# Bulk transfers held until the planner's account of the queue is short: order on SP, and what follows from it

## The chip, the cores and the metric

The kernel runs on one core of a Trainium2 chip. Its engines are TensorE (PE; PEld is its weight load), VectorE (DVE), ScalarE (ACT), GpSimd (POOL) and SyncE (SP), which here issues nearly all transfers. The metric is the device time of one execution in microseconds, the median of several runs; lower is better.

## The reference

Attention whose scores are mixed over the heads before and after the softmax, then one expert layer:

```
scores = q @ k^T / 8                  # batch 4, 12 heads, 448 positions, head size 64
scores = mix over heads (w_pre)
attn   = softmax(scores)
attn   = mix over heads (w_post)
x      = attn @ v                     # 1792 tokens x 768
h      = x @ w_in                     # 768 x 2048
g      = h * clip(h + 3, 0, 6) / 6
out    = g @ w_out                    # 2048 x 768
```

All inputs are float32. w_in and w_out come as 64-bit words and are decoded on the chip.

## The kernel before

**Attention.** The query rows of a batch are cut into 8 tiles m of 60 rows (32 tiles in all). For a tile, three *score products* (line 448, p = 0 to 2) write a pair of PSUM banks, of which there is one; ACT empties it into a tile s (line 473), and SP copies s in four transfers (line 480) into T, where the heads lie side by side. Even m go to T_two, odd m to T_one. Then steps of ten rows follow, numbered s = 0 to 179 (45 a batch) and mostly taken two at a time under the first one's number. Such a step has a *pre mix* of T on PE (line 533), the negative maximum nb on DVE (line 541), the exponential e with its sum on ACT (line 542), the scaling by the sum on POOL, a split of e into two float16 parts eh and el (ACT, POOL), the *post mix* on PE (line 570, 48 matmuls), and the writing of its result into AR by ACT and DVE. After every twelve of them or so comes the *product with v* (line 607), which gives x for the next tokens. PE has six single banks for everything else than the score products.

**The expert layer.** The tokens make eight groups G of 240 or 208. For a group, 16 products of x with w_in (line 828, 18 matmuls each, in the program mostly chained to blocks of 72) give g: ACT (line 841) and DVE (line 843) evacuate, and SP stores two of them at a time from a ring of three tiles to a buffer in DRAM (line 846, gd). These *MoE blocks* are put between the steps of attention.

**w_out.** From step 72 on, every four steps one of 24 pieces of w_out (512 KB) is loaded into a ring of two (`bulk`), decoded by ACT and DVE in a ring WF of four places, and combined with others into seven sums P1 to P7, each stored to DRAM (`w_store`, lines 778 and 781). The last stage (line 1109) loads these sums and g again and makes seven products in place of eight.

**What sets the order.** The program first collects all operations with an engine, a duration, the tiles they read and write, and a priority (smaller goes first). `Plan.schedule` then plays them through: an engine that is free takes, of the operations whose inputs are ready at that time, the one of lowest priority. For a transfer it keeps an account of the queue: `bw["SP"]` is the time at which all that is queued will have moved, at 302 GB/s, and the landing is that time plus a latency. The resulting order is what the program issues. On the chip each engine runs its instructions in this order and waits for the semaphores of their inputs only; no times of the planner exist there.

Priorities that matter: a score copy has about the first step of the tile before its own, less 6; a load of w_out has its step plus 8, keys, queries and v of a batch lie between 30 steps before its first and one behind it; a g store has 20 for the first seven groups and a store of a w_out sum its step plus 10 or 11. So a g store stood ahead of every score copy of a later step.

Of the kernel before, what the change touches and what calls it, by code (L numbers as in the profile page):

```python
# [63 lines left out]
Z_AT = 30  # L64
LAT_0, ACT_T = 1.0, 1
S_BUFS, LAT_T, LAT_B = 3, 2.0, 3.0


class Op:
    __slots__ = ("eng", "dur", "fn", "prio", "n", "succ", "order", "ready", "end", "bytes", "no", "mode", "takes", "then", "share", "lat", "st")  # L70


class Buf:
# [46 lines left out]
class Plan:  # L120
# [11 lines left out]
    def __init__(self):  # L132
        self.ops, self.bufs, self.filler = [], {}, None

    def op(self, eng, dur, fn, r=(), w=(), prio=0.0, after=(), nbytes=0, mode=0, share=False, lat=1.0, st=None):
        o = Op()
        o.lat, o.st = lat, dur if st is None else st
        o.share = share or eng == "POOL"
        o.eng, o.dur, o.fn, o.prio, o.bytes, o.mode = eng, dur, fn, prio, nbytes, mode
        o.succ, o.order, o.n, o.ready, o.no, o.end, o.takes, o.then = [], [], 0, 0.0, len(self.ops), None, [], None  # L140
        deps = {}

        def need(d):
            deps[d.no] = d

        for x in r:
            b, key = x if isinstance(x, tuple) else (x, None)
            for k, u, wr in b.uses:
                if wr and (k is None or key is None or k == key):
                    need(u)  # L150
        for x in w:
            b, key = x if isinstance(x, tuple) else (x, None)
            if b.pool and not b.uses and b not in o.takes:
                o.takes.append(b)
            if b not in self.bufs:
                self.bufs[b] = []
            self.bufs[b].append(o)
            for k, u, wr in b.uses:
                if k is None or key is None or k == key:
                    need(u)  # L160
        for u in after:
            need(u)
        for x, wr in [(x, False) for x in r] + [(x, True) for x in w]:
            b, key = x if isinstance(x, tuple) else (x, None)
            b.uses.append((key, o, wr))
        for d in deps.values():
            d.succ.append(o)
            o.n += 1
        self.ops.append(o)
        return o  # L170
# [14 lines left out]
    def schedule(self, prio, stay):  # L185

        free, wait, ready, out = {}, {}, {}, []
        bw, mode, then = {"SP": 0.0, "ACT": 0.0}, None, None
        recent = collections.deque([(0.0, 0.5, 0.5)], 60)
        for o, n in zip(self.ops, self.counts):  # L190
            o.n, o.ready, o.end = n, 0.0, None
        for p in self.places:
            p.held = [None] * len(p.makes)
        port = {"DVE": 0.0, "POOL": 0.0}

        def push(o):
            if o.eng == "PE":
                ready["PE"].append((prio[o.no], o.no, o))
            else:
                heapq.heappush(wait[o.eng], (o.ready, o.no, o))  # L200

        for o in self.ops:
            if o.eng not in free:
                free[o.eng], wait[o.eng], ready[o.eng] = 0.0, [], []
            if o.n == 0:
                push(o)

        def release(s, t):
            s.ready = max(s.ready, t)
            s.n -= 1  # L210
            if s.n == 0:
                push(s)

        def avail(o):
            t = o.ready
            for p in {b.pool for b in o.takes}:
                x = p.ready(sum(b.pool is p for b in o.takes), self.HOP)
                if x is None:
                    return None
                t = max(t, x)  # L220
            return t

        while True:
            best = None
            for e in free:
                if e == "PE":
                    at = [(avail(x[2]), x) for x in ready[e]]
                    at = [(x, z) for x, z in at if x is not None]
                    if not at:
                        continue  # L230
                    t = max(free[e], min(at)[0])
                elif ready[e]:
                    t = free[e]
                elif wait[e]:
                    t = max(free[e], wait[e][0][0])
                else:
                    continue
                if best is None or t < best[0]:
                    best = (t, e)
            if best is None:  # L240
                break
            t, e = best
            if e == "PE":
                at = [(avail(x[2]), x) for x in ready[e]]
                at = [x for z, x in at if z is not None and z <= t + 1e-9]
                x = min(at)
                x = min([z for z in at if z[2] is then] or [z for z in at if z[2].mode == mode and z[0] < x[0] + stay] or [x])
                then = x[2].then
                ready[e].remove(x)
                o = x[2]  # L250
                fill = self.filler(free[e], t, recent, o) if self.filler else (0, None, 0.0)
                for b in o.takes:
                    b.pool.take(b, self.HOP)
            else:
                while wait[e] and wait[e][0][0] <= t + 1e-9:
                    o = heapq.heappop(wait[e])[2]
                    heapq.heappush(ready[e], (prio[o.no], o.no, o))
                o = heapq.heappop(ready[e])[2]
            o.end = t + o.dur
            if o.share:  # L260
                other = port["POOL" if e == "DVE" else "DVE"]
                o.end += self.SHARE[e] * max(0.0, min(o.dur, other - t))
                port[e] = o.end
            if e == "PE":
                n, fn, z = fill
                if fn is not None:
                    out.append((free[e], fn))
                o.end += z
                recent.append((free[e], t + z, self.FILL * n))
                recent.append((t + z, o.end, o.st))  # L270
            if e == "PE":
                o.end += self.SWITCH * (mode not in (None, o.mode))
                mode = o.mode
            free[e] = o.end
            if o.bytes:
                x, d, other = max(bw[e], t + 1.1), o.bytes / self.DMA_RATE, "ACT" if e == "SP" else "SP"
                both = min(d, max(0.0, bw[other] - x))
                bw[e], bw[other] = x + d + both, bw[other] + both
                o.end = bw[e] + o.lat
            out.append((t, o))  # L280
            for s in o.order:
                release(s, t)
            for s in o.succ:
                release(s, o.end + (0.0 if s.eng == o.eng == "PE" else self.PE_HOP if o.eng == "PE" else self.HOP))
        if sum(isinstance(o, Op) for _, o in out) < len(self.ops):
            return None, out
        return max(o.end for o in self.ops), out
# [17 lines left out]
def body(ctx: ExitStack, tc: tile.TileContext, q4, kT, vj, wpre0, wpost0, ident0, w_in, w_out, outT):  # L305
    nc = tc.nc
    PE, ACT, DVE, POOL, SP = nc.tensor, nc.scalar, nc.vector, nc.gpsimd, nc.sync
# [14 lines left out]
    plan = Plan()  # L322
# [20 lines left out]
    def pe(dur, fn, r, w, prio, after=(), mode=0, st=None):  # L343
        return plan.op("PE", dur, fn, r, w, prio, after, 0, mode, st=st)

    def dma(nbytes, fn, r, w, prio, after=()):
        return plan.op("SP", 0.5, fn, r, w, prio, after, nbytes)

    def dmas(nbytes, out, src, w, prio, after=()):
        return plan.op("SP", 0.5, lambda: SP.dma_start(out(), src), [], w, prio, after, nbytes)  # L350

    def bulk(nbytes, out, src, w, prio, after=()):
        q = BULK
        return plan.op(q, 0.5 if q == "SP" else 0.4, lambda: (SP if q == "SP" else ACT).dma_start(out(), src), [], w, prio, after, nbytes, lat=LAT_B)

    def amax(dst, src):
        DVE.tensor_reduce(dst, src, axis=AX.X, op=ALU.max, apply_absolute_value=True)
# [417 lines left out]

    def w_store(name, i, t, at):
        d = ws_dram[name, i] = Buf(lambda: dram.tile([P, 4 * P], F32, name=f"wsd_{name}_{i}"))
        dma(262144, lambda: SP.dma_start(d(), t()), [t], [d], at)

    def w_sum(out, x, y, op, at):  # L780
        dve(0.69, lambda: DVE.tensor_tensor(out(), x(), y(), op=op), [x, y], [out], at, True)
# [28 lines left out]
    g_dram = [Buf(lambda b=b: dram.tile([P, NFC, S], F32, name=f"gd_{b}")) for b in range(B)]  # L810

    def moe1(G, fcs):
        b, gi = divmod(G, 2)
        n, t0 = GTOK[gi], 240 * gi
        x = x_sb[G]
        at = 5000 + 100 * G
# [3 lines left out]
        for fc in fcs:  # L820
# [12 lines left out]
            r = lambda gt=gt, fc=fc: gt()[:, fc % 2, :n]  # L833
# [10 lines left out]
                                                                                op0=ALU.min, op1=ALU.mult), [ps, (six, fc)], [(gt, fc % 2)], -80)  # L844
            if fc % 2:
                dma(P * 8 * n, lambda fc=fc, gt=gt: SP.dma_start(g_dram[b]()[:, fc - 1:fc + 1, t0:t0 + n], gt()[:, :, :n]), [gt],
                    [(g_dram[b], (fc // 2, gi))], 20 if G < 7 else -500)

# [264 lines left out]
    def out(b, m, half, o):  # L1115
        e = m
        dma(P * 4 * NH, lambda: SP.dma_start(outT[e * P:(e + 1) * P, b * S + half * NH:b * S + half * NH + NH], o()), [o], [], 20)
# [111 lines left out]
```

## Time and profile before

| | |
|---|---|
| median of 3 runs | 797.99 us (795.62 to 799.82) |
| profiled execution, its own time | 803.97 us |
| its span | 802.2 us |
| mean granted TensorE clock | 0.991 |
| PE busy | 779.3 us (97%) |
| PEld busy | 631.3 us (79%) |
| DVE / ACT / POOL busy | 580.3 / 528.1 / 367.7 us |
| moved | 147.75 MB, mean 184 GB/s |
| score copies, issued by SP | 186 to T_two, 240 to T_one |

PE is busy when any matmul is in flight; matmuls overlap, and their ends are modelled. Each engine works in its program order, so an instruction that waits holds all behind it on its engine. Attention with the MoE blocks in it runs until about 580 us, the last stage from there to the end; the stretches of the next-to-last section are chosen along this line. The granted clock is TensorE's, as a share of its full speed.

### The profile page before, as it was taken

To read this page: it belongs to the slowest core of one execution; us is meant where nothing else is said; L and a number is where in the kernel's file an instruction comes from. 1 tells how busy PE (TensorE), PEld (TensorE's weight loads), DVE (VectorE), ACT (ScalarE), POOL (GpSimd) and SP (SyncE) were. 2 spreads that over 40 slices of the span, in tenths; PEclk is the share of its full clock that TensorE was granted. 3 is DMA by queue.
4 is the path that set the end of the run, shared out by engine and by line. 5 is a ranking of instruction groups with operands and counts; after the bars stand their busy time and mean duration, and the time that the engine had idled before them with its cause. 6 is when DMAs were issued, how large, how long until landed. Compare 5 with 4: busy or idle time off the path is not lost.

```text
span 802.2 us, 28025 instructions
## 1 busy us (share of the span) xinstructions
PE 779.3 (97%) x11616; PEld 631.3 (79%) x11616; DVE 580.3 (72%) x1152; ACT 528.1 (66%) x1044; POOL 367.7 (46%) x535
## 2 busy tenths in 40 slices
PE   6999999999999999999999989999999999999998
PEld 2566576577677768777788758768999999999998
DVE  2798886688969357778856776785678688989622
ACT  2487888698998647988775785886577465324200
POOL 2357789579988316777552665766200000000000
PEclk9999999999999999999999998999999999999999
DMA  7866653676364577665657666643699855654101
GB/s 231 228 185 188 200 173 107 217 235 206 96 188 152 160 226 250 221 187 171 206 164 255 202 199 208 188 126 119 180 287 364 292 170 175 187 170 146 41 14 52
DMA packets 100815, 147.75 MB, mean 184 GB/s; under 512 B 9840, under 2 KB 79824, under 8 KB 100688
## 3 DMA queue, kind: packets, MB, share of 16 engines
q1 hardware_dynamic: 100268, 145.31, 58.5%
q8 instruction: 91, 1.49, 0.8%
q10 hardware_dynamic: 420, 0.65, 0.3%
q14 instruction: 36, 0.29, 0.1%
HBM read 76.02 MB, written 31.20 MB: 134 GB/s over the span
## 4 chain that ended last, share of the span: by engine, by line
PE 77%; DVE 7%; DMA 5%; ACT 5%; POOL 2%; issue 2%; SPq 2%; ACTq 0%; POOLq 0%; DVEq 0%
PE single L1109 24%; PE single L828 21%; PE single L570 9%; PE single L607 8%; PE pair L448 7%; PE single L533 6%; PE single L873 3%; DVE nb L541 2%; DMA T_two<-s 2%; ACT e L542 1%; DMA wo<-in_w_out 1%; POOL e L551 1%; DMA T_one<-s 1%; ACT s L473 1%; SPq L480 1%
## 5 line engine op out<-in xcount | busy, mean ns | idle before, releaser
L828 PEld LDWEIGHTS <-wi 128*128 128x128 f16 x2304 | 213.0, 98 | 24.0 <-issue 18.3
L828 PE MATMUL single<-x,wi 128*128 128x208 f16 (+1 forms) x2304 | 228.6, 259 | 1.0 <-DVE AR L579 0.6
L554 POOL TENSOR_TENSOR el<-e,eh 128x448 f16<-128x448 f32 x156 | 166.9, 1089 | 41.5 <-ACT eh L553 39.7
L551 POOL TENSOR_SCALAR e<-e,r 128x448 f32<-128x448 f32 x180 | 129.4, 729 | 38.7 <-DVE r L545 29.4
L1109 PEld LDWEIGHTS <-ws_P 128*128 128x128 f16 x1440 | 138.0, 98 | 0.0
L542 ACT ACTIVATE e<-single,nb 128x448 f32<-128x448 f32 x180 | 113.7, 640 | 26.3 <-DVE nb L541 25.6
L541 DVE TENSOR_REDUCE nb<-single 128x1 f32<-128x448 f32 x180 | 103.5, 615 | 19.1 <-PE single L533 13.5
L841 ACT ACTIVATE g<-single,three,uh 128x240 f32<-128x240 f32 (+1 forms) x128 | 69.3, 542 | 50.9 <-PE single L828 50.3
L553 ACT ACTIVATE eh<-e 128x448 f16<-128x448 f32 x156 | 87.5, 583 | 14.3 <-POOL e L551 13.7
L448 PE MATMUL pair<-ks,qx 64*64 64x448 f32 x728 | 88.8, 552 | 4.5 <-ACT s L473 4.5
L473 ACT ACTIVATE s<-pair 128x896 f32<-128x896 f32 x90 | 82.7, 918 | 14.6 <-PE pair L448 7.8
L843 DVE SCALAR_TENSOR_TENSOR g<-g,six,single 128x240 f32<-128x240 f32 (+1 forms) x128 | 56.3, 442 | 39.9 <-ACT g L841 39.0
L570 PEld LDWEIGHTS <-eh 60*128 60x128 f16 x2496 | 66.2, 100 | 22.2 <-issue 21.0
L607 PEld LDWEIGHTS single<-AR,v 128*64 128x64 f32 (+1 forms) x1536 | 70.4, 140 | 14.2 <-issue 6.3
L607 PE MATMUL single<-AR,v 128*64 128x120 f32 (+3 forms) x1536 | 76.0, 270 | 0.7 <-ACT e L542 0.5
L570 PE MATMUL single<-wpost_h,eh 60*128 60x60 f16 x1248 | 72.2, 202 | 0.2 <-DVE x L633 0.2
L570 PE MATMUL single<-wpost_h,el 60*128 60x60 f16 x1248 | 72.2, 202 | 0.0
L570 PE MATMUL single<-wpost_l,eh 60*128 60x60 f16 x1248 | 71.9, 202 | 0.0
L1109 PE MATMUL single<-gx_P,ws_P 128*128 128x224 f16 x720 | 69.3, 259 | 0.0
L579 DVE TENSOR_SCALAR AR<-single 128x480 f32<-128x480 f32 (+1 forms) x92 | 58.2, 640 | 14.8 <-PE single L570 14.5
L581 ACT ACTIVATE AR<-single 128x480 f32<-128x480 f32 (+1 forms) x92 | 53.6, 585 | 22.5 <-PE single L570 22.0
L544 POOL TENSOR_SCALAR sm<-sm 128x2 f32<-128x2 f32 (+1 forms) x92 | 26.1, 284 | 84.3 <-ACT e L542 79.0
(240 smaller groups left out, 1161.4 us busy)
## 6 DMA issues: line engine op xcount, KB each, us to landing
T_two<-s SPq DMA_DIRECT2D x186, 105.0 KB
T_one<-s SPq DMA_DIRECT2D x144, 105.0 KB
wi<-in_w_in SPq DMA_DIRECT2D x16, 768.0 KB
wo<-in_w_out SPq DMA_DIRECT2D x24, 512.0 KB
wsd_P<-WF SPq DMA_DIRECT2D x42, 256.0 KB
wP<-wsd_P SPq DMA_DIRECT2D x36, 256.0 KB
gd<-g SPq DMA_DIRECT2D x32, 240.0 KB
gd<-g SPq DMA_DIRECT2D x32, 208.0 KB
```

What stands on the lines that cost most here:

```text
L448: PE.matmul(at[u]()[cc * D:cc * D + D], q()[r, o:o + D], ks_[cc]()[r, pr % 3, :], start=True, stop=True)
L473: act(0.9, lambda: ACT.activation(st(), two()[:, :, :S], AF.Copy), ps, [(st, 0), (st, 1)], at + 0.5)
L541: dve(0.53, lambda r=r: DVE.tensor_reduce(nb()[:, r:r + 1], ps[r]()[:, :S], axis=AX.X, op=ALU.max, negate=True), [ps[r]], [(nb, r)], s + 0 ...
L542: act(0.62, lambda r=r: ACT.activation(e()[:, r], ps[r]()[:, :S], AF.Exp, bias=nb()[:, r:r + 1], accum_out=sm()[:, r:r + 1]), [ps[r], (nb, ...
L551: pool(0.63, lambda r=r: POOL.tensor_scalar(e()[:, r], e()[:, r], rr()[:, r:r + 1], 1.0, op0=ALU.mult, op1=ALU.mult), [rr], [(e, r)], s + ...
L553: act(0.47, lambda r=r: ACT.activation(eh()[:, r], e()[:, r], AF.Copy), [(e, r)], [(eh, r)], s + 0.65 + 0.3 * r)
L554: pool(1.02, lambda r=r: POOL.tensor_tensor(el()[:, r], e()[:, r], eh()[:, r], op=ALU.subtract), [(e, r), (eh, r)], [(el, r)], s + 0.7 + 0 ...
L570: PE.matmul(out, x()[rows, r, js], z()[rows], start=(i == 0), stop=(i == len(mix) - 1))
L607: PE.matmul(pss[run]()[u * D:(u + 1) * D, k:k + N], v()[rows, jc, g * D:(g + 1) * D], cols(jc * H + g, rows), start=start, stop=stop)
L828: PE.matmul(pv(), wi_g[g]()[:, w, f0, cc, :], x()[:, z, cc, :n], start=(cc == 0 and i == 0), stop=(cc == 5 and i == 2))
L841: act(0.44, lambda fc=fc, pv=pv, r=r: ACT.activation(r(), pv(), AF.Relu, bias=three()[:, fc:fc + 1], scale=uh()[:, fc:fc + 1]), [ps, (thre ...
L1109: PE.matmul(ps()[:, :NH], w_view(w, y, 2 * m + i)[:, f], g(x)[:, f, :], start=(i == 0 and f == 0 and (y, x) == (0, 0)), stop=(i == 1 and f ...
```

## The change

An operation may carry a `hold` in microseconds. When the planner is about to take it, and the account says that the queue will still be at work for more than `hold` beyond the usual start of a transfer (1.1 us), it is put back to the time at which only `hold` is left; others that are ready go in the meantime. Both holds are 2.0 us. HOLD_IN goes to loads by `bulk` of priority over 100: keys, queries and v of later batches and the later pieces of w_out. HOLD_OUT goes to all stores of w_out's sums and to the g stores of the first seven groups. Nothing else changes, and the chip sees a new order of the same instructions.

```diff
+HOLD_IN, HOLD_OUT, HOLD_AT = 2.0, 2.0, 100
...
                 o = heapq.heappop(ready[e])[2]
+                if o.hold is not None and bw[e] > t + 1.1 + o.hold:
+                    heapq.heappush(wait[e], (bw[e] - 1.1 - o.hold, o.no, o))
+                    continue
             o.end = t + o.dur
...
-    def dma(nbytes, fn, r, w, prio, after=()):
-        return plan.op("SP", 0.5, fn, r, w, prio, after, nbytes)
+    def dma(nbytes, fn, r, w, prio, after=(), hold=None):
+        return plan.op("SP", 0.5, fn, r, w, prio, after, nbytes, hold=hold)
...
     def bulk(nbytes, out, src, w, prio, after=()):
         q = BULK
-        return plan.op(q, 0.5 if q == "SP" else 0.4, lambda: (SP if q == "SP" else ACT).dma_start(out(), src), [], w, prio, after, nbytes, lat=LAT_B)
+        hold = HOLD_IN if prio > HOLD_AT else None
+        return plan.op(q, 0.5 if q == "SP" else 0.4, lambda: (SP if q == "SP" else ACT).dma_start(out(), src), [], w, prio, after, nbytes, lat=LAT_B, hold=hold)
...
-        dma(262144, lambda: SP.dma_start(d(), t()), [t], [d], at)
+        dma(262144, lambda: SP.dma_start(d(), t()), [t], [d], at, hold=HOLD_OUT)
...
-                    [(g_dram[b], (fc // 2, gi))], 20 if G < 7 else -500)
+                    [(g_dram[b], (fc // 2, gi))], 20 if G < 7 else -500, hold=HOLD_OUT if G < 7 else None)
```

The diff adds six lines, so that the lines of the changed kernel have numbers higher by up to six. Three places show what moves.

First, DVE's order before the maximum of step 90 (nb_90), the first step of batch 2. g_2_8 is the ring tile for products 8 and 9 of group 2, wo_13 a piece of w_out, WF the place of its decode, AR the result of a post mix. The kernel before:

```order
L579 TENSOR_SCALAR AR_373<-single2_147 128x48x5
L687 SCALAR_TENSOR_TENSOR WF_195<-wo_13_5111,WF_195 128x512
L691 SCALAR_TENSOR_TENSOR WF_195<-wo_13_5111,WF_195 128x512
L843 SCALAR_TENSOR_TENSOR g_2_8_5444<-g_2_8_5444,six_272,single4_154 128x240
L843 SCALAR_TENSOR_TENSOR g_2_8_5444<-g_2_8_5444,six_272,single1_137 128x240
L843 SCALAR_TENSOR_TENSOR g_2_10_5487<-g_2_10_5487,six_272,single0_85 128x240
L781 TENSOR_TENSOR WF_195<-WF_195 128x512
L843 SCALAR_TENSOR_TENSOR g_2_10_5487<-g_2_10_5487,six_272,single5_156 128x240
L541 TENSOR_REDUCE nb_90_5503<-single2_147 128x1
```

The changed kernel, from the last product of the MoE block before:

```order
L849 SCALAR_TENSOR_TENSOR g_2_6_5294<-g_2_6_5294,six_272,single1_137 128x240
L585 TENSOR_SCALAR AR_373<-single0_85 128x48x10
L585 TENSOR_SCALAR AR_373<-single2_147 128x48x5
L547 TENSOR_REDUCE nb_90_5400<-single4_154 128x1
L547 TENSOR_REDUCE nb_90_5400<-single1_137 128x1
L547 TENSOR_REDUCE nb_92_5417<-single5_156 128x1
```

The decode of w_out, the sum of line 781 and the evacuation of a whole MoE block have moved behind the maxima of batch 2's first steps; on PE the MoE block itself has moved behind the pre and post mix of step 90.

Second, PE's order at the end of the last product with v of batch 2 (AR, v_2). The pair bank is the score products' own. The kernel before:

```order
L607 MATMUL single0_85<-AR_373,v_2_5619 64x90
L607 MATMUL single5_156<-AR_373,v_2_5619 64x90
L448 MATMUL pair0_117<-ks_3_1_7753,qx_3_1_8159 64x448 x4
L533 MATMUL single3_149<-T_one_105,wpre8_107 64x448 x2
L533 MATMUL single4_154<-T_one_105,wpre8_107 64x448 x2
```

The changed kernel:

```order
L613 MATMUL single3_149<-AR_373,v_2_5514 64x90
L613 MATMUL single5_156<-AR_373,v_2_5514 64x90
L834 LDWEIGHTS wi_1_1679
L834 MATMUL single1_137<-x_4_6532,wi_1_1679 128x240
L834 LDWEIGHTS wi_1_1679
L834 MATMUL single1_137<-x_4_6532,wi_1_1679 128x240
```

Of the MoE block that now follows, two of 72 matmuls are shown; behind it come the post mixes of steps 135 and 137, and then the score product.

Third, SP's order before the score copies of tile 24 (s_24_2, the first tile of batch 3). wsd are stores of w_out's sums, wo loads of w_out, gd stores of g, qx a load of queries. The kernel before:

```order
L354 DMA qx_3_1_8159<-in_q4 128x724
L846 DMA gd_2_7572<-g_4_8_8124 128x2x240
L778 DMA wsd_P4_3_8184<-WF_195 128x512
L778 DMA wsd_P5_3_8186<-WF_195 128x512
L778 DMA wsd_P1_3_8190<-WF_195 128x512
L354 DMA wo_7_8240<-in_w_out 128x512
L778 DMA wsd_P7_3_8243<-WF_195 128x512
L354 DMA wo_20_8294<-in_w_out 128x512
```

After these comes one more g store, and then the four copies of s_24_2. The changed kernel, from the copies of s_24_1 on:

```order
L486 DMA T_two_96<-s_24_1_7854 10x6x448
L784 DMA wsd_P3_2_7991<-WF_195 128x512
L852 DMA gd_2_7993<-g_4_0_7962 128x2x240
L486 DMA T_two_96<-s_24_1_7854 10x6x448 x3
L360 DMA qx_3_1_8024<-in_q4 128x724
L360 DMA wo_19_8031<-in_w_out 128x512
L852 DMA gd_2_7993<-g_4_2_8014 128x2x240
L486 DMA T_two_96<-s_24_2_8033 10x6x448
L486 DMA T_one_105<-s_25_0_7966 10x6x448 x4
L486 DMA T_two_96<-s_24_2_8033 10x6x448 x3
```

Fewer bulk transfers stand ahead of s_24_2, and two stores stand between the first copy of s_24_1 and the other three.

## Rows read from the trace of the kernel before

**Rows 1.** Busy time by stretch: length, busy us (instructions) by engine, clock, DMA share, GB/s.

```profile
160.00:285.00 125.00, 122.59 (x2171) 93.55 (x2171) 93.61 (x209) 107.38 (x228) 97.33 (x142) 1.00 0.57 177
285.00:520.00 235.00, 228.32 (x4025) 177.84 (x4024) 169.50 (x353) 176.98 (x387) 139.84 (x185) 0.98 0.66 206
...
560.00:802.00 242.00, 239.08 (x2617) 237.01 (x2615) 171.86 (x264) 101.81 (x143) 6.44 (x15) 1.00 0.55 172
```

**Rows 2.** The same view of two short stretches; columns PE, PEld, DVE, ACT, POOL.

```profile
300.00:305.00 5.00, 4.68 (x54) 4.13 (x52) 3.03 (x8) 4.91 (x14) 2.62 (x5) 0.67 0.94 321
480.00:485.00 5.00, 4.89 (x40) 3.50 (x42) 3.05 (x8) 2.84 (x8) 1.99 (x4) 0.50 0.64 216
```

**Rows 3.** Timeline of PE: start, length, instruction, [idle before, releaser].

```profile
287.58 7.55 PE L828 MATMUL single<-x,wi 128*128 128x240 f16 x72
...
299.57 0.97 PE L533 MATMUL single<-T_two,wpre 60*64 60x448 f32 x4 [1.28 <-DVE g L843]
300.87 1.49 PE L607 MATMUL single<-AR,v 128*64 128x120 f32 x20 [0.32 <-ACT e L542]
...
448.71 0.98 PE L448 MATMUL pair<-ks,qx 64*64 64x448 f32 x8 [1.38 <-ACT s L473]
...
473.95 0.98 PE L448 MATMUL pair<-ks,qx 64*64 64x448 f32 x8
474.76 1.69 PE L533 MATMUL single<-T_two,wpre 64*64 64x448 f32 x16
476.26 0.94 PE L448 MATMUL pair<-ks,qx 64*64 64x448 f32 x8
480.11 1.77 PE L533 MATMUL single<-T_one,wpre 64*64 64x448 f32 x8 [2.92 <-DMA T_two<-s]
```

**Rows 4.** The chain of waits that ended last: start, length, what.

```profile
293.50 4.93 DMA wsd_P<-WF
...
300.87 5.58 PE single L607 x72
...
337.08 3.84 PE single L607 x72
...
463.07 0.96 PE single L570 x48
464.02 0.91 PE single L533 x8
...
480.11 1.77 PE single L533 x8
481.88 5.88 PE single L607 x72
...
548.01 4.62 PE single L607 x96
```

**Rows 5.** Timeline of DVE at step 90.

```profile
298.45 0.69 DVE L781 TENSOR_TENSOR WF<-WF 128x512 f32<-128x512 f32 x1 [4.08 <-DMA wsd_P<-WF]
...
299.44 2.21 DVE L541 TENSOR_REDUCE nb<-single 128x1 f32<-128x448 f32 x4
```

**Rows 6.** Timeline of SP: issues of transfers, a wait for the producer included.

```profile
278.74 2.82 SPq L846 DMA_DIRECT2D gd<-g  x1
...
285.73 2.33 SPq L480 DMA_DIRECT2D T_two<-s  x3
...
289.02 0.42 SPq L846 DMA_DIRECT2D gd<-g  x1
...
293.50 0.44 SPq L778 DMA_DIRECT2D wsd_P<-WF  x1
...
477.01 0.77 SPq L480 DMA_DIRECT2D T_one<-s  x1
```

**Rows 7.** SP's own waits: total us, times, longest.

```profile
SPq L846 <- DVE g L843: 27.2, 21, 2.8
```

**Rows 8.** Waits of the engines: the same columns.

```profile
DVE WF L781 <- DMA wsd_P<-WF: 9.4, 5, 4.1
```

More of the change, by code (lines that the diff above doesn't have):

```diff
@@ L66 @@
 S_BUFS, LAT_T, LAT_B = 3, 2.0, 3.0
+HOLD_IN, HOLD_OUT, HOLD_AT = 2.0, 2.0, 100
 class Op:
-    __slots__ = ("eng", "dur", "fn", "prio", "n", "succ", "order", "ready", "end", "bytes", "no", "mode", "takes", "then", "share", "lat", "st")
+    __slots__ = ("eng", "dur", "fn", "prio", "n", "succ", "order", "ready", "end", "bytes", "no", "mode", "takes", "then", "share", "lat", "st", "hold")
 class Buf:
@@ L133, in __init__, with op @@
         self.ops, self.bufs, self.filler = [], {}, None
-    def op(self, eng, dur, fn, r=(), w=(), prio=0.0, after=(), nbytes=0, mode=0, share=False, lat=1.0, st=None):
+    def op(self, eng, dur, fn, r=(), w=(), prio=0.0, after=(), nbytes=0, mode=0, share=False, lat=1.0, st=None, hold=None):
         o = Op()
+        o.hold = hold
         o.lat, o.st = lat, dur if st is None else st
```

## The prediction

> **What bounds the kernel now.** I read the busy time by stretch first, then TensorE's (PE's) own sequence where it stood idle, then the chain of waits backwards from there, and last VectorE's (DVE's) and SP's sequences at those places. The first thing to see is how little PE stands idle. Up to the post mix that ends at 287.6 us the two orders of PE are the same (SP's differ from m = 8 on, by a few g stores), so I look behind it. From 285 to 520 us PE is busy 228.32 of 235 us, and from 560 on 239.08 of 242, there with its weight loads busy 237.01 as well [rows 1]. The last stage is therefore full, and its order of work is the same in both kernels. What the change can win lies between 285 and 520 us: 235 - 228.32 = 6.68 us of idle PE, plus what PE loses by running at the lower of its two clock levels behind an idle stretch. The granted clock was 0.67 in 300:305 and 0.50 in 480:485 [rows 2]; that is partly or wholly the 1.2 GHz level, after PE had waited 1.60 and 2.92 us.
>
> PE's sequence names three places [rows 3]. The first is at 299 us: a pre mix of T_two waits 1.28 us and the product with v after it 0.32 us. The second is at 448.71: a score product waits 1.38 us for ScalarE (ACT) to empty the pair bank. The third is at 480.11: the pre mix of T_one waits 2.92 us for its score copies. The rest is 6.68 - 1.60 - 1.38 - 2.92 = 0.78 us in small pieces.
>
> Clock loss is the difference between equal work at two levels, from the chain [rows 4]. The product with v of 72 matmuls takes 5.58 us at 300.87 and 5.88 at 481.88, against 3.84 at 337.08; the eight pre matmuls take 1.77 us at 480.11 against 0.91 at 464.02. So the first place costs 1.60 + (5.58 - 3.84) = 3.34 us, the second 1.38, the third 2.92 + (5.88 - 3.84) + (1.77 - 0.91) = 5.82. Together 10.54 us.
>
> **The change, part by part.** It adds, removes and resizes no instruction: both kernels have 17155 rows on PE and the same transfers. What it costs or wins is order alone. On the chip nothing holds a transfer: SP issues in its order and waits only for the producers. So "held" means "behind other things in SP's order", and through the planner's clock other orders on PE, DVE and ACT.
>
> *First place.* In the kernel before, PE does a block of 72 mixture-of-experts (MoE) matmuls, 7.55 us from 287.58 [rows 3], before the pre mix of step 90, and DVE decodes two pieces of w_out and starts a sum meanwhile. That sum (L781) stands ahead of the maximum of step 90 in DVE's order, and waits for a w store issued at 293.50 that takes 4.93 us to land; DVE starts it at 298.45, the maximum at 299.44 [rows 4, 5]. ACT, the product with v and the banks follow from that. In the changed order nothing of w_out stands between the block of g and the maximum of step 90, so this wait has nothing to hold up, and the 3.34 us go. What is late next is T_two itself, since the pre mix now comes right after the post mix that ends at 287.6, without 7.55 us of cover. Its last three copies were issued until 285.73 + 2.33 = 288.06, behind a g store that held SP for 2.82 us [rows 6]; a plain one took 0.42 at 289.02. With that store and one w store (0.44 us at 293.50) behind them they are issued until about 288.06 - 2.82 - 0.44 = 284.8. The nearest row of landing is the last copy of the third place, issued until 477.01 + 0.77 = 477.78 and waited for until 480.11 [rows 3, 6]: 2.3 us. That gives 287.1, no wait. By the w store's 4.93 us it is 289.7, a wait of 2.1 us. I take 0, since these are the same copies, and keep 2.1 for the range. The MoE block is not lost: it goes behind the next pre mixes, and stays one block in hand as cover until the last batch.
>
> *Second place.* PE waits there because two score products follow each other over one pair bank with only the short product with v between them, and ACT comes late to empty the bank [rows 3]. The changed order puts 72 MoE matmuls, about 7.5 us, directly behind that product, and the next score product after two further post mixes. That hides a wait of 1.38 us with room to spare: minus 1.38.
>
> *Third place.* The last score product for T_one starts at 473.95 and its pre mix could start at 480.11: 6.16 us for evacuation, four copies and landing. PE had only 477.20 - 473.95 = 3.25 us of other work [rows 3]. In the changed order there lie between them the score product itself (0.98), 16 pre matmuls (1.69), a score product, a post mix (0.96), a score product, the whole product with v (4.62) and a score product [rows 3, 4]: 0.98 x 4 + 1.69 + 0.96 + 4.62 = 11.2 us against 6.16. The wait goes even if the copies start 5 us later: minus 5.82.
>
> *What the new order adds.* New short waits must be expected, because these three places are only those where this plan was too sure. The nearest rate is that of 160:285, the same mix of work without w_out: 125 - 122.59 = 2.41 us idle at full clock [rows 1], 0.0193 per us, so 4.5 us in 235. The bounds are 0 (no new wait beside the 0.78 that I leave) and, above, the rival on SP below. I take the rate, so 4.5 - 0.78 = 3.7 new.
>
> *The queue itself.* Held loads of w_out come later, so their decodes and stores do. I cost that at nothing: DVE is busy 169.5 of 235 us there [rows 1], the last piece (11) keeps its place near the end of the scores, and PE's cover is the MoE work of the seventh group. If that cover went, the last stage would wait for one late transfer, 4.93 us by the w store's landing [rows 4].
>
> Sum: -10.54 + 3.7 = -6.8 us. The profiled execution took 803.97 us (span 802.2), so 797.2; against the median of 797.99 the same difference gives 791.2.
>
> The Trainium skill, "DMA: Bandwidth & Descriptors", section "Anatomy of one DMA", says that DMA engines do not wait on semaphores: any wait happens on the sequencer that issues, before dispatch. That speaks against the change, because a store moved between score copies makes them wait for the store's producer; this trace agrees, with 27.2 us of such waits. The same skill, "Perfetto Trace Analysis", section "Identifying the Most-Contended Engine", wants PE's headroom read from weight loads, not matmul time; by it 235 - 177.84 = 57 us would be open in 285:520. I go by the pieces of the chain, whose lengths repeat (0.96, 3.84) whatever stands before them.
>
> **Rivals.**
> *All of it.* No new wait: 797.99 - 10.5 = 787.5. For it: one block more in hand, and shorter queues ahead of the copies. Against: no long stretch but 320 to 440 us ran without idle PE.
>
> *The waits move.* The three go, others of the same price come: 797.99 give or take 2. For it: the third wait was a matter of PE's order, not of the queue, because the copies landed 2.3 us after issue; such accidents fall anew in every plan. Then 10.5 us come back in places that no row of before shows.
>
> *Slower: SP held between copies.* The changed order puts w and g stores between the four copies of one score tile more often (at m=24 a w_out sum's store and a g store stand between the first copy and the other three). A store whose DVE result is late holds the copies behind it. Price: SP waited for g 27.2 us in 21 cases [rows 7], 2.8 at the longest, and one such delay that reaches PE costs as the third place does, up to 5.82 us. DVE also has its own wait for w stores, 9.4 us in 5 [rows 8]. With the old three gone (-10.54), two such delays beside the 3.7 give 798 + 4.8 = 802.8, three 808.6. It decides from two on. Against it: after the hold fewer bulk bytes stand in the queue ahead of those copies (at m=24 one load and one g store in place of two loads, four w stores and two g stores).
>
> *The change does nothing on the chip*, because copies were not late by the queue: this is the second rival's time.
>
> **Chances.** Forecast (789 to 794) 0.40, all of it or more (below 789) 0.14, waits that move (794 to 802) 0.29, slower by SP 0.17. About 0.5%, 4 us, is what a measurement here can tell from no change, so the line lies at 794.0 and 802.0: faster 0.54, same 0.29, slower 0.17. The range goes from 785.5 (all of it, 2 us of spread) to 803 (two SP delays); about 0.13 lie above and 0.04 below. The likeliest case's own range is 787 to 794.
>
> **What would show it.** Right: at the pre mix of step 90 PE waits under 1 us, the clock stays at 1.00 in the 5 us after it, the sum L781 no longer stands before a maximum; no idle PE behind the last product with v of batch 2; the pre mix of T_one in batch 3 without a wait; the last stage begins some 7 us earlier with the same length. Wrong: idle PE above 5 us between 285 and 560, most of all behind score copies that SP issued late after a wait for DVE; or a last stage that grows because w_out comes late.

## The result, and the profile after

The changed kernel took 801.62 us (median of 10 runs, 798.43 to 807.33), the kernel before 797.6 (10 runs beside it, 794.0 to 799.91): the ratio is 1.0058, with a 95% interval of 1.0036 to 1.0081. A repeat gave 1.0026 (0.9995 to 1.0057), which alone would not exclude equal times. So the change makes the kernel slower by some 0.3 to 0.6%, where I had forecast 0.85% faster. The time lies inside the range given, the direction was wrong. Ratios, here and below, leave out executions in the slower of the kernel's two states and need not be the quotient of the medians given.

The profiled execution of after took 803.02 us (span 801.2, clock 0.995), of the same length as the profiled one of before, 803.97. That already warns: among its own fellows the profiled execution of before was a long one, above all ten runs timed beside the result.

Busy time by stretch, after, with the columns of [rows 1]:

```profile
160.00:285.00 125.00, 122.39 (x2168) 92.60 (x2161) 94.46 (x210) 107.78 (x230) 97.60 (x142) 1.00 0.56 171
285.00:520.00 235.00, 230.98 (x4056) 177.81 (x4056) 178.72 (x359) 180.66 (x393) 148.52 (x190) 0.99 0.68 210
...
560.00:801.00 241.00, 238.14 (x2611) 236.60 (x2608) 168.05 (x251) 101.30 (x142) 5.49 (x10) 1.00 0.54 171
```

Between 285 and 520 us PE is idle 235 - 230.98 = 4.02 us, less than the 6.68 of [rows 1] (other executions, below, differ: 6.98 in a repeat of after, 3.90 and 4.31 in two of before). The last stage begins with the first product of line 1115 at 579.10 us and ends with the span: 801.2 - 579.10 = 222.1 us. Before it was 802.2 - 580.08 = 222.1 too. So nothing came out of the last stage in either direction; it began 1.0 us earlier, where some 7 had been forecast.

The first place, step 90, in PE's timeline of after (start, length, instruction, idle before and its releaser):

```profile
288.62 0.19 PE L576 MATMUL single<-wpost_h,el 60*128 60x60 f16 x2
290.74 0.98 PE L539 MATMUL single<-T_two,wpre 64*64 64x448 f32 x8 [1.93 <-DMA T_two<-s]
291.51 1.18 PE L454 MATMUL pair<-ks,qx 64*64 64x448 f32 x8
292.38 3.29 PE L539 MATMUL single<-T_two,wpre 64*64 64x448 f32 x16
295.60 3.91 PE L613 MATMUL single<-AR,v 128*64 128x120 f32 x72
```

The post mix ends at 288.8, and now nothing covers T_two: 1.93 us of waiting. Then the same 16 pre matmuls that took 1.69 us in [rows 3] take 3.29; the clock of 290:295 shows why (columns as in [rows 2]):

```profile
290.00:295.00 5.00, 4.26 (x32) 1.78 (x32) 1.92 (x4) 3.14 (x9) 0.19 (x1) 0.71 0.67 199
295.00:300.00 5.00, 5.00 (x84) 4.02 (x84) 1.79 (x5) 3.62 (x10) 4.27 (x7) 0.95 0.76 245
```

By starts that follow one another at full clock, the pre, the score product and the 16 pre matmuls want about 0.87 + 0.80 + 1.50 = 3.2 us (462.31 to 463.18 and 471.51 to 472.31 in the next fence, 474.76 to 476.26 in [rows 3]); here they took 295.60 - 290.74 = 4.86. Wait and clock together cost 1.93 + 1.7 = 3.6 us, as much as the 3.34 of the old first place. The second and third places, however, are clear:

```profile
436.94 7.55 PE L834 MATMUL single<-x,wi 128*128 128x240 f16 x72
446.23 0.98 PE L454 MATMUL pair<-ks,qx 64*64 64x448 f32 x8
...
462.31 0.93 PE L539 MATMUL single<-T_two,wpre 64*64 64x448 f32 x8
463.18 6.59 PE L834 MATMUL single<-x,wi 128*128 128x208 f16 x72
...
471.51 0.98 PE L454 MATMUL pair<-ks,qx 64*64 64x448 f32 x8
472.31 1.69 PE L539 MATMUL single<-T_two,wpre 64*64 64x448 f32 x16
474.18 0.98 PE L454 MATMUL pair<-ks,qx 64*64 64x448 f32 x8 [0.18 <-ACT s L479]
...
477.11 4.69 PE L613 MATMUL single<-AR,v 128*64 128x120 f32 x96
...
482.37 0.93 PE L539 MATMUL single<-T_one,wpre 60*64 60x448 f32 x8
```

At the second place the block of 72 matmuls at 436.94 and the post mixes now lie before the score product of 446.23, which does not wait. The score products of the third place wait 0.18 us at most, and the pre mix of T_one (482.37) stands behind the product with v without a wait, as forecast.

SP at the first place, in after: issues, waits between the issues of a group included, to set beside [rows 6]:

```profile
276.77 1.30 SPq L360 DMA_DIRECT2D wo<-in_w_out  x2
278.18 0.78 SPq L486 DMA_DIRECT2D T_two<-s  x1
279.06 3.28 SPq L486 DMA_DIRECT2D T_one<-s  x4
282.38 5.55 SPq L486 DMA_DIRECT2D T_two<-s  x3
```

And the chain of waits that ends in that pre mix (start, length, what):

```profile
276.77 7.77 DMA wo<-in_w_out
...
284.56 5.44 DMA T_two<-s
290.00 0.73 issue
```

The g store of 2.82 us is gone, as the order said, but three copies that took 2.33 us in [rows 6] now take 5.55. The s pieces that they copy were finished by 280.2 (ACT's last write of s there starts at 279.24 and takes 0.92); the chain names a load of w_out that landed at 284.54. SP's own waits from 274 to 290 us say the same (total us, times, longest), and the three copies one by one show where the two waits are:

```profile
SPq L486 <- DMA wo<-in_w_out: 3.3, 2, 1.9
```

```profile
282.38 0.75 SPq L486 DMA_DIRECT2D T_two<-s  x1
...
284.56 0.75 SPq L486 DMA_DIRECT2D T_two<-s  x1
...
287.18 0.75 SPq L486 DMA_DIRECT2D T_two<-s  x1
```

What ties the copies to loads into other tiles stands in the trace's instructions. Each transfer that SP issues reports its landing on one of eight semaphores, which come round in turn here, and SP first waits for the same semaphore, that is, until the transfer eight places before has landed. The second and third of these copies stand eight places behind the two loads of w_out. The loads' last landing updates came at 284.54 and 287.16, and the copies were issued 0.02 us after each. So it is a wait that the program contains, and it goes with the place in SP's order.

### The profile page after: what moved, and what is told of

Same layout as the page of the kernel before. It is cut to its first block, busy times and chain, and to the rows that moved or that the text cites. A ratio compares the mean times of both kernels' runs of the same rounds, so it can differ in the third digit from the quotient of the medians.

```text
span 801.2 us, 28022 instructions
## 1 busy us (share of the span) xinstructions
PE 779.9 (97%) x11616; PEld 629.4 (79%) x11616; DVE 585.3 (73%) x1152; ACT 529.0 (66%) x1044; POOL 374.2 (47%) x535
## 4 chain that ended last, share of the span: by engine, by line
PE 40%; DMA 9%; DVE 5%; ACT 5%; POOL 3%; SPq 3%; issue 2%; ACTq 0%; POOLq 0%; DVEq 0%
PE single L1115 24%; PE single L834 10%; DMA wsd_P<-WF 3%; DMA T_two<-s 3%; ACT e L548 2%; SPq L486 2%; POOL el L560 2%; PE pair L454 2%; PE single L576 2%; PE single L613 2%; DVE nb L547 1%; PE single L539 1%; ACT eh L559 1%; DMA wo<-in_w_out 1%; DMA v<-in_vj 1%
## 5 line engine op out<-in xcount | busy, mean ns | idle before, releaser
L560 POOL TENSOR_TENSOR el<-e,eh 128x448 f16<-128x448 f32 x156 | 170.6, 1112 | 24.2 <-ACT eh L559 21.8
L454 PE MATMUL pair<-ks,qx 64*64 64x448 f32 x728 | 90.5, 554 | 3.2 <-ACT s L479 3.1
L613 PEld LDWEIGHTS single<-AR,v 128*64 128x64 f32 (+1 forms) x1536 | 66.6, 136 | 13.3 <-issue 6.7
L613 PE MATMUL single<-AR,v 128*64 128x120 f32 (+3 forms) x1536 | 72.3, 263 | 0.2 <-DVE AR L585 0.2
```

The source lines that it names most:

```text
L454: PE.matmul(at[u]()[cc * D:cc * D + D], q()[r, o:o + D], ks_[cc]()[r, pr % 3, :], start=True, stop=True)
L560: pool(1.02, lambda r=r: POOL.tensor_tensor(el()[:, r], e()[:, r], eh()[:, r], op=ALU.subtract), [(e, r), (eh, r)], [(el, r)], s + 0.7 + 0 ...
L613: PE.matmul(pss[run]()[u * D:(u + 1) * D, k:k + N], v()[rows, jc, g * D:(g + 1) * D], cols(jc * H + g, rows), start=start, stop=stop)
```

## Experiments

Stretches below (attention from step 90 on) run from the start of the post mixes before step 90 to the first product of the last stage: 293.8 us in the profiled execution of before, 291.7 in after.

**Another execution of before, and one of after.** No edit.

> The kernel before, unchanged, for a second profile. Theory A (the profiled execution of before was not typical: it took 803.97 us where others took 794 to 799.9): the idle PE between 285 and 520 us is 3 us or less instead of 6.68, the clock stays near 1.00, and at least one of the three waits (1.60, 1.38, 2.92 us) is missing; span about 796. Rival B (the three waits are in every execution, and the changed kernel lost the time elsewhere): the same three waits to within 0.5 us.

> The changed kernel, unchanged, beside the mixtures below on the same chip. Ratio to before 1.003 to 1.009, as measured first (1.0058). The wait of 1.93 us before the pre mix of step 90 is there again (over 1.5 us) if it comes from the order, and gone if it was an accident of one execution.

The kernel before took 795.4 us in this execution (span 793.6), its stretch 286.9. PE was idle 235 - 231.10 = 3.90 us from 285 to 520, somewhat above the 3 expected, at a clock of 1.00. Its three places:

```profile
297.27 0.97 PE L533 MATMUL single<-T_two,wpre 60*64 60x448 f32 x4 [0.62 <-DVE g L843]
298.56 3.91 PE L607 MATMUL single<-AR,v 128*64 128x120 f32 x72 [0.32 <-ACT e L542]
...
474.28 0.98 PE L533 MATMUL single<-T_one,wpre 64*64 64x448 f32 x8 [0.21 <-DMA T_one<-s]
475.19 3.91 PE L607 MATMUL single<-AR,v 128*64 128x120 f32 x72
```

The same order of the same instructions, and the first place costs 0.62 + 0.32 = 0.94 us in place of 3.34 (the product with v takes 3.91, so no clock was lost), the third 0.21 in place of 5.82. Only the second is as it was: 1.39 us.

The repeat of after took 800.36 us against 796.97, a ratio just under the range expected; the stretch of its profiled execution is 295.2. Step 90 there:

```profile
287.60 1.77 PE L539 MATMUL single<-T_two,wpre 64*64 64x448 f32 x8 [3.74 <-DMA T_one<-s]
...
293.50 3.91 PE L613 MATMUL single<-AR,v 128*64 128x120 f32 x72
```

A wait of 3.74 us and 293.50 - 287.60 = 5.90 in place of 3.2: 6.4 us in all. The new wait is there in both executions, the old third one isn't. The releaser named here is a copy of the other tile, but the last copy of T_two landed at 287.30, 0.3 us before the pre mix, as it did in after (290.44). The three copies of T_two were issued from 278.69 for 4.11 us, until 282.80.

**A third execution of the kernel before.** No edit.

> The kernel before once more, a third profile. By theory A (the profiled execution of the forecast was not typical) the wait for score copies at the third place is under 1 us as in the second profile, and the clock stays at 1.00 behind it; the wait of some 1.4 us for ACT at the second place is there in all three, since it comes from the order.

800.78 us, stretch 289.2:

```profile
301.28 0.97 PE L533 MATMUL single<-T_two,wpre 60*64 60x448 f32 x4 [1.64 <-DVE g L843]
302.58 5.58 PE L607 MATMUL single<-AR,v 128*64 128x120 f32 x72 [0.33 <-ACT e L542]
...
479.58 0.98 PE L533 MATMUL single<-T_one,wpre 64*64 64x448 f32 x8
480.49 3.91 PE L607 MATMUL single<-AR,v 128*64 128x120 f32 x72
```

The first place costs 1.64 + 0.33 and clock again (the product takes 5.58; the granted clock was 0.83 in 300:305): 1.97 + (5.58 - 3.84) = 3.7. The second is 1.38 again, the third nothing. So the old places cost 10.54, 2.5 and 5.1 us in three executions (0.94 + 1.39 + 0.21, and 3.7 + 1.38), 6.1 in the mean. These three took 800.1 us in the mean, above the medians of 797 to 798, so 6.1 is high rather than low.

**Orders mixed.** In mix_sp the planner runs for both kernels, and SP's sequence is taken from after, so far as its tiles allow, with the other engines' of before; in mix_rest the other way round.

```diff
+SP_HELD, REST_HELD = True, False   # mix_sp; mix_rest: False, True
...
+        sp = [o for o in order(SP_HELD) if isinstance(o, Op) and o.eng == "SP"]
+        rest = [o for o in order(REST_HELD) if not isinstance(o, Op) or o.eng != "SP"]
```

> Both plans are made; PE, DVE, ACT and POOL keep the order of the kernel before, and SP issues in the held order, as far as the other orders allow it. Theory S (SP's order costs: stores between score copies hold the copies): ratio 1.004 or more, near the changed kernel. Rival P (the new order of the compute engines costs, above all pre mixes that come without a MoE block before them): 0.998 to 1.002. If the held order on the queue is good by itself, as the change means it: 0.995 or below.

> The other mixture: PE, DVE, ACT and POOL in the changed kernel's order, SP in that of the kernel before, as far as the others allow it. Theory S: 0.998 to 1.002. Rival P: 1.004 or more; more than the changed kernel if its order needs the held queue, because the copies for step 90 then come later still (a wait over 3 us there).

891.46 us, ratio 1.1197 (1.1136 to 1.1258), and 937.92, ratio 1.1757 (1.1703 to 1.181). Neither theory had that. They say nothing on the 0.5% in question: SP's sequence is the other plan's only as far as the tiles allow, and 12 and 18% drown any merit of either order. Where the time goes in them is left open.

**One hold alone.**

```diff
-HOLD_IN, HOLD_OUT, HOLD_AT = 2.0, 2.0, 100
+HOLD_IN, HOLD_OUT, HOLD_AT = 2.0, None, 100   # in_only
+HOLD_IN, HOLD_OUT, HOLD_AT = None, 2.0, 100   # out_only
```

> HOLD_OUT is None: only bulk loads of priority over 100 are held, stores go as before. PE's order is that of before until step 135, with the MoE block in front of the pre mix of step 90. Theory N (what the change costs is mainly the new wait in front of that pre mix, 1.93 and 3.74 us in two executions, which the held stores bring by taking the MoE block away): ratio 0.997 to 1.002, no wait over 0.7 us there. Rival L (held loads of w_out come late, and their decodes then stand before the maxima on DVE, at 320 to 330 and 440 to 460 us): 1.003 to 1.008.

> HOLD_IN is None: only stores are held. PE takes the pre mix of step 90 right behind the post mix of step 89, as in the changed kernel. Theory N: ratio 1.003 to 1.008, and a wait over 1.5 us for score copies in front of that pre mix. Rival L: 0.997 to 1.002.

in_only: 795.68 us, ratio 0.9994 (0.9963 to 1.0024). out_only: 803.82, ratio 1.0057 (1.0023 to 1.0092), the whole change's own ratio. So the hold on stores carries the loss, and the hold on loads neither helps nor harms by more than 0.4%. PE's largest waits of out_only, 285 to 560 us (total us, times, longest):

```profile
PE single L539 <- DMA T_two<-s: 1.6, 1, 1.6
PE single L539 <- DVE WF L787: 1.2, 1, 1.2
PE single L834 <- DVE x L639: 0.9, 1, 0.9
```

The first is step 90 again, at 285.45, this time without a loss of clock. That execution took 797.1 us, the shortest of its twelve, so its waits show where a loss can arise and not the median's loss. In in_only the MoE block stands before that pre mix as in before, and PE's waits there, 0.9 us at the longest, are for POOL, ACT and DVE, none for a copy.

**The cover given back.** If the loss is the wait at step 90 and no more, a kernel with the block of 72 matmuls back in front of it must win it back. The planner moves the block back when its account lets the copies of tile 16 land 4 us later:

```diff
-lat=LAT_T if m else LAT_0
+lat=(LAT_T + (4.0 if m == 16 else 0.0)) if m else LAT_0   # lat16
-S_BUFS, LAT_T, LAT_B = 3, 2.0, 3.0
+S_BUFS, LAT_T, LAT_B = 3, 4.0, 3.0   # lat4: all tiles
```

> The changed kernel, with 4 us more latency in the planner's account for the score copies of tile 16 alone, so that the plan puts a MoE block between the post mix of step 89 and the pre mix of step 90 again. The rest of the plan moves with it. Theory N: the wait in front of that pre mix is under 0.5 us, ratio 0.996 to 1.001. If the loss is spread over the whole stretch (theory W: waits of the same price come elsewhere, wherever the plan is too sure), 1.003 or more, with the wait at step 90 gone all the same.

> The changed kernel with LAT_T 4.0 in place of 2.0: the account gives all score copies 2 us more to land, so that every pre mix is planned later and more MoE blocks stand in front of them. Theory N and W alike: waits of PE for T are under 1 us in total between 285 and 560 us; by N the ratio is 0.992 to 1.000. If later plans only move the wait to the maxima and to ACT (rival: the copies' landing is not what the plan is wrong about), 1.000 to 1.010.

lat16: 803.61 us, ratio 1.0083 (1.0055 to 1.0112). The pre mix of step 90 no longer waits for T_two (those below are at other steps), and nothing is won. PE's waits moved:

```profile
PE single L613 <- ACT e L548: 1.9, 2, 1.0
PE single L539 <- issue: 1.7, 1, 1.7
...
PE single L539 <- DMA T_two<-s: 1.3, 1, 1.3
PE pair L454 <- ACT s L479: 1.0, 1, 1.0
```

The theory that step 90 alone is the loss fell here. lat4: 816.97 us, ratio 1.0243 (1.0203 to 1.0283), beyond what either theory had. With every copy planned 2 us later no wait for a copy is among PE's largest any more; it waits for ACT (2.5 us for s, 1.5 and 1.1 for e), and idles already before the stretch of the change:

```profile
160.00:285.00 125.00, 116.92 (x2124) 87.12 (x2119) 94.24 (x212) 104.53 (x219) 99.23 (x142) 0.99 0.52 156
```

125 - 116.92 = 8.1 us idle, against 2.41 in [rows 1].

**Which stores.**

```diff
-        dma(262144, lambda: SP.dma_start(d(), t()), [t], [d], at, hold=HOLD_OUT)
+        dma(262144, lambda: SP.dma_start(d(), t()), [t], [d], at)   # no_w
-    20 if G < 7 else -500, hold=HOLD_OUT if G < 7 else None)
+    20 if G < 7 else -500)   # no_g
```

> The changed kernel without the hold on the stores of w_out's sums; loads and g stores stay held. PE does a score product and then eight plus eight pre matmuls right behind the post mix of step 89, again without a MoE block. Theory W (any plan that counts on early copies behind the two unheld w_out loads takes the MoE block away and waits): ratio 1.002 to 1.010, a wait over 1 us for the copies of tile 16. If only the held w stores cost: 0.997 to 1.002.

> The changed kernel without the hold on the g stores; loads and w stores stay held. The same place is planned as in the run without held w stores. Theory W: ratio 1.002 to 1.010, a wait over 1 us for the copies of tile 16. If only the held g stores cost: 0.997 to 1.002.

no_w (g stores alone held): 806.02 us, ratio 1.0105 (1.0056 to 1.0154). no_g (sums' stores alone held): 800.76, ratio 1.0008 (0.997 to 1.0045). PE's largest waits, no_w and then no_g:

```profile
PE pair L454 <- ACT s L479: 3.3, 4, 2.1
PE single L576 <- POOL el L560: 1.9, 3, 1.0
```

```profile
PE pair L454 <- ACT s L479: 2.6, 2, 2.3
```

Theory W had both slower; only no_w is, so holding the g stores is the costlier half: the two intervals do not touch. In both the longest of these waits stands at step 90 again, one instruction earlier: its score product (288.91 and 288.79) waits for ACT, which waited (1.01 and 2.80 us) for a score copy before it could write s. So the plans without one of the holds keep a wait for copies there, and the same wait in no_g goes with a ratio near 1. By how much either hold costs I don't say; the intervals of no_g and of the whole change overlap.

**One load fewer ahead of the copies.** With HOLD_AT at 75 the second of the two loads of w_out is held behind them.

```diff
-HOLD_IN, HOLD_OUT, HOLD_AT = 2.0, 2.0, 100
+HOLD_IN, HOLD_OUT, HOLD_AT = 2.0, 2.0, 75
```

> The changed kernel with HOLD_AT 75 in place of 100: the first w_out loads are held as well, so that one of them, not two, stands ahead of the last copies of tile 16. PE still does the pre mix of step 90 without a MoE block. If the copies are late there because SP's issue is held until the w_out loads have landed (5.55 and 4.11 us for three copies that take 2.33 otherwise): the wait there is under 1 us, and the ratio 0.996 to 1.003. If they are late for another reason: over 1.5 us, 1.003 or more.

799.58 us, ratio 1.0017 (0.9983 to 1.0052). SP still stood at the copies, less than in after, and PE still waited at step 90. SP's wait, SP's timeline and PE's wait:

```profile
SPq L486 <- DMA wo<-in_w_out: 1.2, 1, 1.2
```

```profile
275.39 0.78 SPq L360 DMA_DIRECT2D wo<-in_w_out  x1
...
280.93 3.46 SPq L486 DMA_DIRECT2D T_two<-s  x3
```

```profile
PE single L539 <- DMA gd<-g: 1.8, 1, 1.8
```

The expected wait of under 1 us did not come: the three copies were issued until 280.93 + 3.46 = 284.39, and the pre mix started at 287.88, 3.5 us later. One load is enough to hold SP: it landed at 282.84, and the copy eight places behind it was issued at 282.85. The wait of 1.79 us cost no clock here (1.00 in 285:290 and in 290:295).

No version beat the kernel before; in_only equals it.

## Why the prediction was wrong

**What held.** That the old three places go, that the last stage keeps its 222.1 us, and that PE is the engine where it is decided. The orders were read rightly as well; what SP waits for in its order was not.

**Failed: the price of the old places, 10.54 us.** It was read off one execution, 6 us above the median. In the others the same order cost 2.5 and 5.1 us there. The second place, 1.38, was there each time (1.38, 1.39, 1.38), as a wait that follows from the order would be: two score products over one pair bank. The third, 5.82, was there once in three. In the mean there were 6.1 us to win, 4.4 fewer than the sum had.

**Failed: "287.1, no wait" at step 90.** I let the copies end at 284.8 by taking out the g store's 2.82 us, and land 2.3 us later. Against the end of the post mix that is 2.8 us before it, and 0.5 in hand. Measured, the copies ended 0.9 us before it in after (287.93 against 288.8) and 1.1 in the repeat (282.80 against 283.9), and PE went on 2.8 and 4.8 us behind their issue: 2.8 - 0.9 = 1.9 and 4.8 - 1.1 = 3.7, the two waits. Both halves were short, the issue by 1.9 and 1.7 us, the landing by 0.5 and 2.5.

The step behind the first half is the premise that SP "waits only for the producers" (the section on the kernel says the same). SP also waits for the transfer eight places before:

| execution | loads issued until | (second) load landed | copy eight places behind it issued | last copy issued until |
|---|---|---|---|---|
| before | 278.64 | 285.77 | 286.52 | 288.06 |
| before, second | 276.66 | 283.50 | 283.51 | 285.05 |
| before, third | 279.74 | 288.38 | 288.40 | 289.94 |
| after | 278.08 | 287.16 | 287.18 | 287.93 |
| after, repeat | 273.96 | 282.04 | 282.05 | 282.80 |
| out_only | 273.87 | 281.76 | 281.78 | 282.52 |
| at75 (one load) | 276.17 | 282.84 | 282.85 | 284.39 |

In [rows 6] that wait was hidden: the g store's 2.82 us delayed the copies until both loads had landed (283.87 and 285.77, the copies behind them issued at 285.73 and 286.52). In the other two executions of before the same store took 0.43 and 0.42 us, and the copies 3.27 and 4.02 instead of 2.33. So taking the store out could not save 2.82 us; the copies could not be issued before the loads had landed. With that in it, my own sum gives 285.77 + 0.75 = 286.5 in place of 284.8, an estimate from the first execution's rows: 1.1 us before the post mix ends, where 0.9 and 1.1 were measured. Why that one g store took 2.82 us stays open. It was not late in its source, for DVE's last write to a g before it is this one, and the next starts at 281.35:

```profile
274.31 0.47 DVE L843 SCALAR_TENSOR_TENSOR g<-g,six,single 128x240 f32<-128x240 f32 x1 [1.38 <-ACT g L841]
```

Then the lower clock was added, which I had reckoned into the old place and not into the new: 3.6 and 6.4 us in all, 5.0 in the mean, against 0 taken and 2.1 as the bound. (It was not added in out_only and at75, where waits of 1.62 and 1.79 us left the clock at 1.00.)

**Not refuted: the other new waits, 3.7 us.** The stretch of after is 293.4 us in the mean of two, that of before 290.0 in the mean of three: +3.4. With 6.1 gone, 9.5 are new; 5.0 of them are step 90, and 4.5, by subtraction, the rest. They are scattered, for instance 1.38 us for T_two at 427 us in the repeat alone. The rate was taken from 160:285 as a stretch without w_out, which it is not: five of its loads are issued there, from 226.8 us on. And the sign that the sum no longer stands before a maximum held at step 90 only: the repeat has it in the chain at another step.

```profile
321.68 1.36 DVE WF L693
...
323.06 1.41 DVE WF L697
...
325.41 0.60 DVE WF L787
...
326.08 2.13 DVE nb L547 x4
```

So the forecast of -6.8 misses by 4.4 + 5.0 + 0.8 = 10.2, and 10.2 - 6.8 = 3.4 us slower, which is what the stretches show and what the two ratios (2.1 and 4.6 us) lie around. The means are of three and two executions that scatter by 7 and 3.5 us, so neither the split nor the difference of 3.4 itself is good to more than a few us.

**The rivals.** "The waits move" is what happened in kind, with a price above the one given: the plans of lat16, no_w and no_g each have new waits, at step 90 or elsewhere. "Slower: SP held between copies" gave nearly the right end (802.8) by a mechanism that was not seen: at step 90 SP was held by the landing of loads, not by a store whose DVE result was late. That the end came out is luck.

**Why holding stores harms.** Shown: out_only alone gives the whole loss, in_only none. Read from the orders, and not shown: with stores out of the account the planner finds the queue short, believes that the copies of tile 16 are early, and takes the MoE block that covered them for later. The two loads ahead have priorities under 100 and are not held. That this is all of the loss is refuted by lat16; why the altered plans cost what they do elsewhere, from 0.1% (no_g) to 2.4% (lat4), stays open. One rival was not tested: the planner adds a random part to every priority (`DRAWS, JITTER = (3,), 0.3`, one fixed draw), and no run changed the draw of the kernel before. So it is not known whether the hold itself costs, or whether most plans that differ from this one would. Left open as well is why the start of the stretch scatters between 282.5 and 287.7 us from one execution to the next.

## What to carry to other kernels

Before a wait's price goes into a sum, look whether the same wait is there in a second execution: one that follows from the order comes back (1.38, 1.39, 1.38 us), one that hangs on a transfer may not (2.92, 0.21, none). When an order loses a store on which the issuing engine stood, look for every wait that stands behind it: here the instructions hold each transfer until the one eight places before has landed, so small copies behind a long load are late whatever else moves. And when a plan takes the cover from in front of a transfer, expect the wait to show (1.93, 3.74 and 1.62 us here), but do not expect a plan that only puts the cover back to win it: lat16 won nothing.

## What the runs showed of the hardware

In this program SP does not issue a transfer before the one eight places ahead, on the same semaphore, has landed: the copies behind the loads of w_out were issued 0.01 to 0.02 us after the loads' last landing update in six executions of the table above (284.54 and 284.56, 287.16 and 287.18 in after), though in after their source had been written 2 us before. In after the two loads took 7.8 and 9.8 us from the start of their issue to their landing. The Trainium skill, "DMA: Bandwidth & Descriptors", section "Anatomy of one DMA", puts waits on the sequencer that issues; the rows agree that the time is spent there.

The clock after an idle stretch is not a fixed toll: idle pieces of 0.62 and 0.32 us cost none (product with v 3.91 us), pieces of 1.64 and 0.33 did (clock 0.83 in 300:305 of the third execution of before). One wait of 1.79 us cost none either (at75, clock 1.00 in 290:295), and one of 1.93 did (after, 0.71 in 290:295). The values between 0.5 and 1 are stretches spent partly at the 1.2 GHz level.
